# Where slab 0's reciprocal root is computed, and in what order the first loads and matmul pieces are asked for

## Chip, core and metric

The kernel runs on one core of one Trainium2 chip. The core has five engines that run their own instruction queues: TensorE (PE in the profile, with its weight loads as PEld), VectorE (DVE), ScalarE (ACT), GpSimd (POOL) and SyncE (SP), whose queue issues the DMAs here. An engine's queue is in order: an instruction that waits holds up all that stand behind it. The metric is the device time of one execution in microseconds (us); three runs of the kernel before lay within 0.02% of each other.

## The reference, cut to what matters

```python
def reference(A_x, A_w_r, A_w_i, B_x, B_w_gate, B_w_up, B_w_down):
    xn = _layernorm(A_x, axis=-1)                       # (1, 2048, 640), eps 1e-5
    s = irfft2(rfft2(xn) * (A_w_r + 1j * A_w_i))        # spectral filter over both axes
    g = _silu((_gelu(xn @ B_w_gate) * (xn @ B_w_up)) @ B_w_down)   # 640 -> 1536 -> 640
    return A_x + s * g
```

All inputs are bf16. The layer norm of each row (640 elements) needs the row's mean and variance, then 1/sqrt(variance + 1e-5).

## The kernel before, in words

The 2048 rows are cut into 16 slabs of 128 rows (slab n1 holds the rows n1, n1+16, ...), each a tile of 128 partitions by 640 elements in the buffer `X`. Four slabs make a group; a group's normalised rows are transposed into `xnT[g]` (five chunks of 128 columns). The feed-forward part runs tile by tile of 128 of the 1536 hidden columns: for tile t a *gate piece* is five matmuls into a PSUM buffer `psg` (one per chunk), which ScalarE turns into `ge` by gelu, and an *up piece* is five matmuls into `psu`, which VectorE multiplies by `ge` into `uT` (line 795). `psg` and `psu` have two buffers each, so the third gate piece in a row can't begin before the gelu of the first has read its buffer, and likewise for up pieces and their products. Afterwards come the down projection (line 814) and, woven between, the spectral part: folds on VectorE, DFT matmuls, and trips through DRAM. The order of all work is written out by hand: a list `back` of feed-forward pieces and a list `plan` of the other work attached to each.

The change touches the first 11 us alone. There, SP's queue asks for the loads in this order: x of slab 0, the gate weights of tiles 0 to 2 (480 KB), x of slab 1 (160 KB), the up weights of tile 0 (160 KB), the up weights of tiles 1 and 2 (320 KB), x of slabs 2 and 3, then further weights. TensorE runs idle matmuls (`warm_pe`, line 590) on a constant tile until data is there: 19 before the first transposes, and two after them. Slab 0 goes through these steps:

- `stats(0)`: two `bn_stats` of 320 columns each (line 183) and a `bn_aggr` (line 188) on VectorE.
- `root(0, 1)`: VectorE adds 1e-5 (`ve`, line 197), GpSimd raises to the power -0.5 (line 199).
- `inv_consts()`: nine tiny VectorE instructions on 128x1 columns (line 255), constants that are used much later.
- `norm_parts(0)`: VectorE normalises 384, then 256 columns (line 205).
- `slab_Tparts(0)`: three, then two transposes on TensorE into a PSUM tile (line 849), and a copy of each part into `xnT` (line 850). Both copies of slab 0 are ScalarE's; of slab 1's, ScalarE has the first and VectorE the second.

`stats(1)` stands between `norm_parts(0)` and the transposes, then `root(1, 1)`, `inv_rest()` (five tiny VectorE instructions that depend on one another) and the first entries of `back`. Written as g0, u0 for the gate and up piece of tile 0, TensorE's order for slab 0 is g0 g1 u0 g2, transposes of slab 1, u1 u2; and for slab 1 g0 g1 u0 g2 u1 u2. From tile 3 on, gate and up pieces cover two slabs at a time (256 columns), in the order g u g u. ScalarE's function table for gelu is loaded by its first instruction (line 215), while nothing else is there to do.

Of the kernel before, what the change touches and what calls it, by code (L numbers as in the profile page):

```python
# [12 lines left out]
ACT = mybir.ActivationFunctionType  # L13
# [19 lines left out]
def kernel(  # L33
# [40 lines left out]
    with tc.manual_schedule():  # L74
        build(nc, locals())


def build(nc, env):
# [5 lines left out]
    def load_x(n0, n, eng=nc.sync):  # L84
        eng.dma_start(out=X[:, n0:n0 + n, :], in_=xv[:, n0:n0 + n, :])

    def load_w(k, t0, t1):
        f0, f1 = t0 * P, t1 * P
        nc.sync.dma_start(out=(Wg, Wu)[k][:, :, f0:f1], in_=(wgv, wuv)[k][:, :, f0:f1])

    def load_gu(t0, t1):
        for k in range(2):
            load_w(k, t0, t1)

    load_x(0, 1)
    load_w(0, 0, 3)
    load_x(1, 1)
    load_w(1, 0, 1)
    load_w(1, 1, 3)
    load_x(2, 2)  # L100
    load_gu(3, 5)
    load_gu(5, 7)
# [63 lines left out]
    def c1(name, dt=FP32):  # L166
        return consts.tile([P, 1], dt, name=name)

    done = set()
    mva = {}  # L170
    rstd = {}
# [7 lines left out]
    def half_stats(n1, k):  # L179
        if k == 0:  # L180
            st_n[n1] = work.tile([P, 2, nc.vector.BN_STATS_DIM], FP32, tag="st", bufs=3, name="st")
        st = st_n[n1]
        nc.vector.bn_stats(out=st[:, k, :], in_=X[:, n1, 320 * k:320 * k + 320])  # L183
        if k == 1:
            g = n1 // 4
            if g not in mva:
                mva[g] = work.tile([P, 4, nc.vector.BN_AGGR_DIM], FP32, tag="mva", bufs=2, name=f"mva{g}")
            nc.vector.bn_aggr(out=mva[g][:, n1 % 4, :], in_=st)

    def stats(n1):  # L190
        for k in range(2):
            half_stats(n1, k)

    def root(n0, n):
        m = mva[n0 // 4][:, n0 % 4:n0 % 4 + n, :]
        ve = work.tile([P, 4], FP32, tag="ve", name="ve")[:, 0:n]
        nc.vector.tensor_scalar(out=ve, in0=m[:, :, 1], scalar1=1e-5, scalar2=None, op0=ALU.add)  # L197
        r = work.tile([P, 4], FP32, tag="rst", bufs=4, name="rst")[:, 0:n]
        nc.gpsimd.tensor_tensor(out=r, in0=ve, in1=mhalf[:, 0:n], op=ALU.pow)  # L199
        rall[n0] = r  # L200
        for k in range(n):
            rstd[n0 + k] = r[:, k:k + 1]

    def norm(n1, c0=0, c1_=D):
        nc.vector.tensor_scalar(out=X[:, n1, c0:c1_], in0=X[:, n1, c0:c1_], scalar1=mva[n1 // 4][:, n1 % 4, 0:1],
                                scalar2=rstd[n1], op0=ALU.subtract, op1=ALU.mult)
        if c1_ == D:
            done.add(("n", n1))
# [3 lines left out]
    negpi = c1("negpi")  # L212
    nc.vector.memset(negpi, -PI_SAFE)
    warm = c1("warm")
    nc.scalar.activation(out=warm, in_=negpi, func=ACT.Gelu_apprx_tanh)
    b_0, b_1 = c1("b_0"), c1("b_1")
    nc.vector.memset(b_0, 320.0)
    nc.vector.memset(b_1, 0.0)
# [34 lines left out]
    def affine(name, src, a, b):  # L253
        t = c1(name)
        nc.vector.tensor_scalar(out=t, in0=src, scalar1=float(a), scalar2=float(b), op0=ALU.mult, op1=ALU.add)
        return t
# [7 lines left out]
    def fma(name, src, k, add, dt=FP32):  # L264
        t = c1(name, dt)
        nc.vector.scalar_tensor_tensor(out=t, in0=src, scalar=float(k), in1=add, op0=ALU.mult, op1=ALU.add)
        return t
# [8 lines left out]
    def times(name, src, k, by):  # L276
        t = c1(name)
        nc.vector.scalar_tensor_tensor(out=t, in0=src, scalar=k, in1=by, op0=ALU.mult, op1=ALU.mult)
        return t
# [18 lines left out]
    def inv_consts():  # L298
        i_0 = affine("i_0", pf, 4.0, 0.0)
        i_1 = affine("i_1", pf, 4.0, 4.0)  # L300
        i_2 = affine("i_2", pf, 4.0, 2.0)
        o_0 = affine("o_0", pf, 2.0, 320.0)
        o_1 = affine("o_1", pf, 2.0, 2.0)
        o_2 = affine("o_2", pf, 2.0, 321.0)
        o_3 = affine("o_3", pf, 2.0, 1.0)
        ab.extend([(i_0, o_0), (i_1, o_1), (i_2, o_2), (i_2, o_3)])
        kc.append(affine("l_s", s_f, 2.0, 256.0))
        kc.append(affine("hk", h_f, -2.0, 1.0))

    def inv_rest():  # L310
        cq, l_s, hk = kc
        l_k = fma("l_k", h_f, 2.0, l_s)
        l_r = fma("l_r", times("lh", hk, 1.0, hi_f), 1.0, l_k)
        i_r = affine("i_r", l_r, 2.0, 0.0)
        o_r = fma("o_r", l_r, 1.0, cq)
        ab.append((i_r, o_r))
# [1 line left out]
    fwd_consts()  # L318
    vt_iota(0)
    stats(0)  # L320
    root(0, 1)
    inv_consts()

    def tinv_phase(h):
        sl = slice(8 * h, 8 * h + 8)
# [260 lines left out]
    def warm_pe(n):  # L586
        if not warm_bank:
            warm_bank.append(bank(0))
        for _ in range(n):
            nc.tensor.matmul(warm_bank[0][:, 0:256], lhsT=ones[:, 0:P], rhs=ones, start=True, stop=True)  # L590
# [180 lines left out]
    def bank(k):  # L771
        return psA.tile([P, 512], FP32, tag="gu"[k], name="ps" + "gu"[k])
# [55 lines left out]
        for t, k in tk:  # L828
            ffn_piece(0, t, k, j * P, j * P + P)

    GG, REST = ((0, 0), (1, 0)), ((0, 1), (2, 0))

    def run(*items):
        for it in items:
# [2 lines left out]
    PARTS = ((0, 3), (3, 5))  # L837

    def norm_parts(n1):
        for a, b in PARTS:  # L840
            norm(n1, a * P, b * P)

    def slab_Tparts(n1):
        if n1 == 0:
            xnT[0] = xg.tile([P, 5, 512], BF16, tag="xg", name="xnT0")
        for (a, b), ev in zip(PARTS, (nc.scalar.copy, nc.scalar.copy if n1 == 0 else nc.vector.tensor_copy)):
            pt = psB.tile([P, 5, P], BF16, tag="b")
            for c in range(a, b):
                nc.tensor.transpose(out=pt[:, c, :], in_=X[:, n1, c * P:(c + 1) * P], identity=ident)
            ev(out=xnT[0][:, a:b, n1 * P:n1 * P + P], in_=pt[:, a:b, :])  # L850
        done.add(("T", n1))

    NP = 8
    back = [(run, (ffn_slab, 0, GG), (norm_parts, 1), (vt_iota, 1), (ffn_slab, 0, REST), (slab_Tparts, 1),
             (ffn_slab, 0, ((1, 1), (2, 1))),
             (half_stats, 2, 0)),
            (run, (ffn_slab, 1, GG + REST[:1]), (half_stats, 2, 1), (root, 2, 1), (ffn_slab, 1, REST[1:])),
            (run, (ffn_slab, 1, ((1, 1), (2, 1))), (norm, 2), (stats, 3), (root, 3, 1))]
    for h in range(2):
        for t in range(0 if h else 3, NP):  # L860
            back.append((ffn_part, 0, t, h))
# [9 lines left out]
    def put(s, *item):  # L871
        plan[s].append(item)

    put(5, norm, 3)
    put(5, slab_T, 2, 1)
    put(6, slab_T, 3, 0)
# [81 lines left out]
    for i, (n0, n) in enumerate(DG):  # L958
        a = vs0 + 7 * i
# [10 lines left out]
            if (n0 + k) % 2 and 1 < (n0 + k + 3) // 2 < 8:  # L970
                put(min(d + (5 + k if n == 3 else 2), vs0 + 41), load_xt, (n0 + k + 3) // 2)

    warm_pe(19)
    norm_parts(0)
    stats(1)
    slab_Tparts(0)
    warm_pe(2)
    root(1, 1)
    inv_rest()

    put(5, phase_const)
# [36 lines left out]
```

## Time and profile before

| | us |
|---|---|
| median of three runs (202.99 to 203.03) | 203.01 |
| the profiled execution | 203.26 |
| its span, first to last instruction | 201.5 |
| TensorE busy in it | 193.4 |
| VectorE busy | 132.2 |
| ScalarE busy | 122.7 |
| GpSimd busy | 37.4 |

The granted TensorE clock was 0.998 of full speed over the span. TensorE is busy 96% of the span; what it is not busy is mostly in the first 15 us. In the profile, an instruction group is named by its line, its engine, its operation and what it writes and reads (`uT<-psu,ge`); a bracket gives the idle time of the engine just before it and what ended that idle time.

### The profile page before, as it was taken

What the parts mean: (1) busy time and instruction counts of PE and PEld (TensorE: products, weight loads), DVE (VectorE), ACT (ScalarE), POOL (GpSimd) and SP (SyncE); (2) the same over time, 40 slices, a digit from 0 to 9 for tenths busy, and PEclk for the clock granted to TensorE, in tenths of its full rate; (3) what the DMA queues carried; (4) which work ended last, traced back from release to release, by engine and by line L of the source; (5) the groups of instructions that cost most, each with busy time, mean ns of one, the idle gap of its engine ahead of it and who ended that gap; (6) DMA issues with size and microseconds to landing.
All of it is one profiled execution on the core that took longest, in us unless ns stands there. A gap on an engine that the chain in (4) does not pass through costs nothing.

```text
span 201.5 us, 4153 instructions
## 1 busy us (share of the span) xinstructions
PE 193.4 (96%) x1534; PEld 118.6 (59%) x1549; DVE 132.2 (66%) x320; ACT 122.7 (61%) x217; POOL 37.4 (19%) x62
## 2 busy tenths in 40 slices
PE   7889999999999997999999999999999999999993
PEld 5678854777555554576643433457765555556773
DVE  7876869799698784132665557423239786878673
ACT  2447657966967763733688787623564757476632
POOL 5427769999001000000000000000000000000000
PEclk9999999999999999999999999999999999999999
DMA  6999998656669537427982022249900406142512
GB/s 170 332 313 305 387 314 166 130 144 241 156 148 149 134 91 307 121 65 223 322 201 85 25 98 98 109 122 276 282 1 27 140 22 206 36 130 45 186 64 69
DMA packets 40325, 32.44 MB, mean 161 GB/s; under 512 B 15088, under 2 KB 38256, under 8 KB 40048
## 3 DMA queue, kind: packets, MB, share of 16 engines
q1 hardware_dynamic: 40304, 32.17, 55.8%
q8 instruction: 12, 0.20, 0.4%
q14 instruction: 9, 0.07, 0.2%
HBM read 19.03 MB, written 7.88 MB: 134 GB/s over the span
## 4 chain that ended last, share of the span: by engine, by line
PE 64%; DVE 1%; issue 1%; ACT 0%; DVEq 0%
PE psu L789 16%; PE psg L789 16%; PE psg L814 10%; PE psu L814 10%; PE pv L706 2%; PE pd L553 2%; PE pu L653 2%; PE px L626 2%; PE pd L574 1%; PE pd L557 1%; PE pz L543 1%; DVE uT L795 0%; PE pd L576 0%; DVE y L479 0%; ACT G L819 0%
## 5 line engine op out<-in xcount | busy, mean ns | idle before, releaser
L789 PE MATMUL psu<-xnT,Wu 128*128 128x512 bf16 (+2 forms) x289 | 61.0, 339 | 0.9 <-DVE uT L795 0.3
L789 PE MATMUL psg<-xnT,Wg 128*128 128x512 bf16 (+2 forms) x286 | 60.4, 338 | 0.8 <-ACT xnT L850 0.2
L795 DVE TENSOR_TENSOR uT<-psu,ge 128x512 bf16<-128x512 f32 (+2 forms) x59 | 34.4, 587 | 27.8 <-PE psu L789 22.1
L793 ACT ACTIVATE ge<-psg 128x512 bf16<-128x512 f32 (+2 forms) x59 | 30.5, 518 | 27.5 <-PE psg L789 24.6
L814 PEld LDWEIGHTS <-uT 128*128 128x128 bf16 x396 | 37.3, 98 | 14.3 <-issue 0.4
L789 PEld LDWEIGHTS <-Wu 128*128 128x128 bf16 x295 | 26.7, 98 | 23.3 <-issue 3.2
L789 PEld LDWEIGHTS <-Wg 128*128 128x128 bf16 x295 | 26.7, 98 | 21.7 <-issue 1.8
L814 PE MATMUL psg<-Wd,uT 128*128 128x320 bf16 (+1 forms) x204 | 30.7, 294 | 0.0
L814 PE MATMUL psu<-Wd,uT 128*128 128x320 bf16 (+1 forms) x192 | 28.7, 296 | 0.0
L638 DVE TENSOR_TENSOR X<-xs,W 128x972 bf16<-128x972 bf16 (+2 forms) x22 | 13.3, 648 | 10.2 <-ACT xs L634 9.3
L579 ACT CAST zd<-pd 128x660 bf16<-128x660 f32 x16 | 11.3, 706 | 5.5 <-PE pd L576 4.3
L183 DVE BATCH_NORM_STATS2 st<-X 128x6 f32<-128x320 bf16 x32 | 14.1, 477 | 0.4 <-DMA X<-in_A_x_dram 0.3
L708 ACT CAST W<-pv 128x640 bf16<-128x640 f32 x16 | 11.1, 695 | 5.0 <-PE pv L706 5.0
L731 ACT ACTIVATE W<-pd 128x960 bf16<-128x960 f32 (+2 forms) x14 | 10.1, 780 | 5.6 <-PE pd L557 5.5
L545 ACT CAST GEN<-pz 128x640 bf16<-128x640 f32 x16 | 11.2, 702 | 3.1 <-PE pz L543 3.1
L659 ACT CAST X<-pu 128x486 bf16<-128x486 f32 (+4 forms) x22 | 12.3, 558 | 0.3
L634 ACT CAST xs<-px 128x972 bf16<-128x972 f32 (+2 forms) x11 | 10.3, 937 | 2.9 <-PE px L626 2.9
L823 DVE SCALAR_TENSOR_TENSOR G<-th,psg 128x320 bf16<-128x320 f32 x8 | 3.9, 488 | 11.4 <-ACT th L822 11.4
L199 POOL TENSOR_TENSOR rst<-ve,mhalf 128x1 f32<-128x1 f32 (+1 forms) x7 | 5.4, 767 | 23.0 <-DVE ve L197 23.0
L737 DVE TENSOR_TENSOR W<-W 128x960 bf16<-128x960 bf16 (+1 forms) x12 | 6.9, 599 | 3.9 <-ACT W L731 3.8
L764 DVE TENSOR_TENSOR Yall<-Yall,G 128x640 bf16<-128x640 bf16 (+3 forms) x19 | 8.2, 434 | 1.6 <-ACT G L819 1.3
L765 DVE TENSOR_TENSOR Yall<-Yall,xt 128x640 bf16<-128x640 bf16 (+3 forms) x19 | 8.3, 439 | 0.7
(134 smaller groups left out, 207.9 us busy)
## 6 DMA issues: line engine op xcount, KB each, us to landing
W<-W SPq DMA_DIRECT2D x4, 642.0 KB, 5.1
ZDR<-zd SPq DMA_DIRECT2D x32, 80.2 KB, 2.6
xt<-in_A_x_dram SPq DMA_DIRECT2D x8, 320.0 KB, 3.8
UDR<-X SPq DMA_DIRECT2D x10, 240.8 KB, 2.5
out_dram<-Yall SPq DMA_DIRECT2D x14, 160.0 KB, 2.4
B<-ZDR SPq DMA_DIRECT2D x8, 240.8 KB, 4.2
W<-UDR SPq DMA_DIRECT2D x4, 481.5 KB, 6.6
X<-in_A_x_dram SPq DMA_DIRECT2D x3, 640.0 KB, 6.9
```

The costliest lines, as they stand in the source:

```text
L183: nc.vector.bn_stats(out=st[:, k, :], in_=X[:, n1, 320 * k:320 * k + 320])
L545: nc.scalar.copy(out=Zt[n1], in_=pz)
L579: nc.scalar.copy(out=zd.rearrange("p c (q e) -> p c q e", e=10), in_=pd[:, :, 0:330].rearrange("p c (e q) -> p c q e", q=33))
L634: nc.scalar.copy(out=xs, in_=px[:, :, 0:n * w].rearrange("p k (h l) -> p k h l", l=w))
L638: nc.vector.tensor_tensor(out=pp[-1], in0=xs, in1=WT[:, :, h0:h0 + n, l0:l0 + w], op=ALU.mult)
L659: nc.scalar.copy(out=us[:, :, :, c0:c0 + (w + 1 - m) // 2], in_=pv[:, :, :, m:w:2])
L708: nc.scalar.copy(out=vs, in_=pv)
L731: nc.scalar.activation(out=eo[:, b, :, a0:a1].rearrange("p k a n -> p a k n"), in_=py[b][:, a0:a1], func=ACT.Copy, scale=(2.0 if silu[a0] ...
L789: nc.tensor.matmul(ps, lhsT=WT[:, c, t * P:(t + 1) * P], rhs=xnT[g][:, c, c0:c1_], start=(c == 0), stop=(c == 4))
L793: nc.scalar.activation(out=ges[t], in_=ps, func=ACT.Gelu_apprx_tanh)
L795: nc.vector.tensor_tensor(out=uT[g][:, t, c0:c1_], in0=ps, in1=ges[t], op=ALU.mult)
L814: nc.tensor.matmul(ph, lhsT=uT[g][:, t, j * P:(j + 1) * P], rhs=Wd[:, t, c0:c1_], start=(t == 0), stop=(t == NT - 1))
```

## The change

1. Loads: x of slab 1 is asked for second, before the gate weights of tiles 0 to 2; the up weights of tiles 0 to 2 come in one transfer of 480 KB, where there were two.
2. Root of slab 0: one ScalarE instruction, `Abs_reciprocal_sqrt` of the variance with 1e-5 as its bias, in place of VectorE's addition and GpSimd's power. ScalarE's first instruction now loads the table for this function, and a one-column gelu right behind the root loads the gelu table. One constant column (`eps`) is new.
3. VectorE's order: the first half of `stats(1)` moves ahead of `norm_parts(0)`, the second half behind the copy of slab 0's first part. `inv_consts()` moves from behind the root of slab 0 to behind the root of slab 1, just before `inv_rest()`.
4. The copies of slab 0: VectorE has the first part (384 columns), ScalarE the second.
5. TensorE's order: slab 0 is g0 g1 g2 u0 u1, transposes of slab 1, u2; slab 1 is g0 g1 g2 u0 u1 u2. 17 idle matmuls stand before the first transposes, five behind them.

```diff
     load_x(0, 1)
-    load_w(0, 0, 3)
     load_x(1, 1)
-    load_w(1, 0, 1)
-    load_w(1, 1, 3)
+    load_gu(0, 3)
     load_x(2, 2)
...
+    def root_act(n1):
+        rstd[n1] = c1("rst0")
+        nc.scalar.activation(out=rstd[n1], in_=mva[n1 // 4][:, n1 % 4, 1:2], func=ACT.Abs_reciprocal_sqrt, bias=eps)
+        nc.scalar.activation(out=warm, in_=negpi, func=ACT.Gelu_apprx_tanh)
...
     warm = c1("warm")
-    nc.scalar.activation(out=warm, in_=negpi, func=ACT.Gelu_apprx_tanh)
+    eps = c1("eps")
+    nc.vector.memset(eps, 1e-5)
+    nc.scalar.activation(out=warm, in_=eps, func=ACT.Abs_reciprocal_sqrt)
...
     stats(0)
-    root(0, 1)
-    inv_consts()
+    root_act(0)
+    half_stats(1, 0)
...
-    GG, REST = ((0, 0), (1, 0)), ((0, 1), (2, 0))
+    GG, UU = ((0, 0), (1, 0), (2, 0)), ((0, 1), (1, 1), (2, 1))
...
-        for (a, b), ev in zip(PARTS, (nc.scalar.copy, nc.scalar.copy if n1 == 0 else nc.vector.tensor_copy)):
+        evs = (nc.scalar.copy, nc.vector.tensor_copy)
+        for (a, b), ev in zip(PARTS, evs[::-1] if n1 == 0 else evs):
...
-    back = [(run, (ffn_slab, 0, GG), (norm_parts, 1), (vt_iota, 1), (ffn_slab, 0, REST), (slab_Tparts, 1),
-             (ffn_slab, 0, ((1, 1), (2, 1))),
+    back = [(run, (ffn_slab, 0, GG), (norm_parts, 1), (vt_iota, 1), (ffn_slab, 0, UU[:2]), (slab_Tparts, 1),
+             (ffn_slab, 0, UU[2:]),
              (half_stats, 2, 0)),
-            (run, (ffn_slab, 1, GG + REST[:1]), (half_stats, 2, 1), (root, 2, 1), (ffn_slab, 1, REST[1:])),
-            (run, (ffn_slab, 1, ((1, 1), (2, 1))), (norm, 2), (stats, 3), (root, 3, 1))]
+            (run, (ffn_slab, 1, GG + UU[:1]), (half_stats, 2, 1), (root, 2, 1), (ffn_slab, 1, UU[1:2])),
+            (run, (ffn_slab, 1, UU[2:]), (norm, 2), (stats, 3), (root, 3, 1))]
...
-    warm_pe(19)
+    warm_pe(17)
     norm_parts(0)
-    stats(1)
     slab_Tparts(0)
-    warm_pe(2)
+    half_stats(1, 1)
+    warm_pe(5)
     root(1, 1)
+    inv_consts()
     inv_rest()
```

## The prediction, made before the result was known

> **What bounds the kernel now.** I read the page first, then the windows by stage, then the timeline of each engine over the first 15 us. The page's first part and the windows (columns: the window, its length, then busy us of PE, PEld, DVE, ACT, POOL, the granted clock, DMA share, GB/s) say where TensorE is not full:
>
> ```profile
> PE 193.4 (96%) x1534; PEld 118.6 (59%) x1549; DVE 132.2 (66%) x320; ACT 122.7 (61%) x217; POOL 37.4 (19%) x62
> ```
>
> ```profile
> 0.00:5.00 5.00, 3.83 (x19) 2.72 (x19) 3.64 (x38) 1.49 (x2) 2.50 (x10) 1.00 0.60 169
> 5.00:15.00 10.00, 8.79 (x103) 7.08 (x102) 8.27 (x32) 4.82 (x14) 3.35 (x8) 1.00 1.10 323
> 15.00:68.00 53.00, 52.42 (x412) 35.01 (x414) 42.91 (x99) 38.42 (x69) 31.07 (x44) 1.00 0.80 211
> ```
>
> From 15 us on TensorE is full (52.42 of 53 us, and 119.39 of 123.5 after 78). So the change is worth what it moves the moment from which TensorE runs without holes. The timeline of PE shows that moment: its last hole is ahead of the up piece at 14.67, and the lines at 8.32, 11.13 and 12.18 wait for VectorE too.
>
> ```profile
> 6.65 0.82 PE L789 MATMUL psg<-xnT,Wg 128*128 128x128 bf16 x10 [0.23 <-ACT xnT L850]
> 8.32 0.54 PE L849 MATMUL pt<-ident,X 128*128 128x128 bf16 x5 [0.29 <-DVE X L205]
> ...
> 11.13 0.44 PE L789 MATMUL psu<-xnT,Wu 128*128 128x128 bf16 x5 [0.31 <-DVE uT L795]
> ...
> 14.67 0.71 PE L789 MATMUL psu<-xnT,Wu 128*128 128x256 bf16 x5
> ```
>
> What the piece at 14.67 needs is a `psu` buffer, which the product of tile 3 gives back. The timeline of DVE shows that product last in one long chain that begins at 10.79:
>
> ```profile
> 7.05 0.15 DVE L197 TENSOR_SCALAR ve<-mva 128x1 f32<-128x1 f32 x1
> ...
> 7.89 0.64 DVE L205 TENSOR_SCALAR X<-X,mva,rst 128x384 bf16<-128x384 bf16 x2
> ...
> 10.79 0.29 DVE L795 TENSOR_TENSOR uT<-psu,ge 128x128 bf16<-128x128 f32 x1 [0.56 <-PE psg L789]
> 10.99 0.48 DVE L183 BATCH_NORM_STATS2 st<-X 128x6 f32<-128x320 bf16 x1
> ...
> 12.59 0.45 DVE L205 TENSOR_SCALAR X<-X,mva,rst 128x640 bf16<-128x640 bf16 x1 [0.27 <-POOL rst L199]
> 12.95 0.88 DVE L183 BATCH_NORM_STATS2 st<-X 128x6 f32<-128x320 bf16 x2
> 13.87 0.21 DVE L188 BATCH_NORM_AGGREGATE mva<-st 128x2 f32<-128x12 f32 x1
> 14.11 0.15 DVE L197 TENSOR_SCALAR ve<-mva 128x1 f32<-128x1 f32 x1
> 14.19 0.76 DVE L795 TENSOR_TENSOR uT<-psu,ge 128x256 bf16<-128x256 f32 x2
> ```
>
> From the first product of slab 1 (10.79) to the end of the first one at 14.19 it is 3.83 us of instructions that the change leaves in their order. **The forecast is therefore the start of slab 1's first product, against 10.79.** What comes earlier counts only as far as it moves that.
>
> **Part by part.** Times are us of the profiled span.
>
> *Root.* Before: aggregate done 4.26, `ve` 0.15, POOL's power 4.53 to 5.11, norm at 5.14. After: ScalarE's 128x1 instruction. Nearest rows: the 128x1 at 2.01 took 0.20; 128x66 with pointers for scale and bias took 0.43 (two in 0.76). I take 0.30, as one pointer lies between: root done 4.60. Meanwhile VectorE runs half of slab 1's statistics (0.48, next slot at 4.59). Norm at 4.63, 0.51 earlier (bounds 4.59 and 4.73). The new `eps` memset (0.06) goes into VectorE's 0.33 of idle time ahead of 3.13.
>
> *Loads.* x of slab 1 landed 4.2 after its issue at 1.65, 0.42 behind the gate weights (1.18 + 4.3). Second in the queue it lands 0.42 behind slab 0's (0.72 + 2.4), near 3.5; at the 177 GB/s that DMA moved from 2 to 3 us it would be 4.0. It is needed at 4.18: hidden. The gate weights now land third with the same bytes as slab 1's x had, 5.86; needed at 6.36. The 480 KB of up weights follow at 291 to 353 GB/s (the windows from 5 to 10 us): 7.3 to 7.5; the two transfers of before ended at 7.78 (2.68 + 5.1). I take 7.45. One issue (0.53 on SP) goes; all behind it on SP moves up, but lands by bytes: x of slabs 2 and 3 (8.6 before) is needed at 9.5.
>
> *Table load behind the root.* It lies on ScalarE between the root and the copy of slab 0's second part. The load at line 793 stands in the timeline of ACT like this:
>
> ```profile
> 51.36 0.71 ACT L545 CAST GEN<-pz 128x640 bf16<-128x640 f32 x1
> 52.09 1.28 ACT L793 ACT_TABLE_LOAD   x1
> 53.38 0.60 ACT L793 ACTIVATE ge<-psg 128x512 bf16<-128x512 f32 x1
> ```
>
> The instruction before ends at 52.07, the next starts 0.01 behind the load: 1.28 in all. After: load 4.60 to 5.89, gelu 0.20, copy (0.38, overlapping by 0.10 as at 6.12) 6.00 to 6.38. VectorE's copy of 384 columns is 0.36 (between 0.29 for 256 and 0.48 for 640): transposes at 5.07 (0.44 behind the norm, as before), copy 5.64 to 5.99. Five idle matmuls hold TensorE to 6.36 (two at 0.21, three at 0.11: the spacing halves at 5.98). So g0 starts 6.36 against 6.65, and passes its fourth chunk at 6.52 against 6.93. The load is covered, with 0.14 to spare. A switch that cost more would delay g0 by the rest, of which 0.26 more is absorbed ahead of slab 1's transposes.
> The Trainium skill, "ScalarE: Activation LUTs", section "What ACT_TABLE_LOAD costs", speaks against this: it adds about 1.38 of drain to the 1.28, some 2.66 a switch. This trace shows the 1.28 and no drain. By the page g0's fourth chunk would come near 7.8 and the sum would be +1.1, where the row gives +0.1.
>
> *Slab 1's statistics and norm.* The second half runs behind VectorE's copy, 5.91 to 6.39, aggregate 6.43, `ve` 6.67 (before 7.05): 0.38 earlier, POOL's result at 7.47. But now all fourteen tiny constants stand between `ve` and the norm. Before, nine (4.36 to 4.99) lay under slab 0's power, and five (7.12 to 7.79) under slab 1's. Together: nine at 0.06, then five with their dependences, last one started 7.82. Norm(1) starts 7.88 against 7.89: the 0.38 is gone. Bounds: 7.48, POOL's result, and 7.95.
>
> *Order of pieces.* A piece is 0.28, a gelu of 128 columns 0.28.
> Slab 0: g0 to 6.64, g1 to 6.91, g2 waits for the gelu of g0 (6.84 to 7.12) until 7.17, u0 7.50 (weights), u1 to 8.05. Transposes of slab 1: 8.31 against 8.32. Behind them u2 needs u0's buffer, whose product runs 8.44 to 8.73 behind the norm: u2 8.79. ScalarE's copy of slab 1 8.68 to 9.16, so g0 of slab 1 at 9.22 against 9.26. The piece that was done ahead is lost again in waiting.
> Slab 1: g1 9.50; g2 must wait for the gelu of g0 (9.70 to 9.98): 10.03, a hole of 0.25 that the old order filled with u0. So u0 runs 10.31 (before 9.82) and is ready at 10.77 (before 10.27); its product, 0.09 later, at 10.86.
>
> *The idle time at 10.79.* VectorE was free at 10.22 and u0 done at 10.27, so this product could have run at 10.34; it ran at 10.79, and the releaser named had nothing to do with it. Counted in the trace it is VectorE's 64th instruction, waits included. If the 0.45 belongs to that place in the queue, the changed kernel passes it near 9.5 to 10.0, while it waits for u0 anyway; that is the nearest reading, since it is the only such idle time on VectorE. If it belongs to this instruction, it is paid again (rival 1).
>
> *Sum.* 10.86 against 10.79, 0.07; the same working applied to the old order comes 0.02 below the trace at this place, so I take +0.10. All of it reaches 14.67 and so the end. Profiled execution 203.26 + 0.10 = 203.36; the median stands 0.25 under that execution, so 203.01 + 0.10 = **203.11**. Under 0.2% (0.41 us) a measurement of this kernel says nothing, so this is "same".
>
> **The rivals.**
> 1. The idle 0.45 follows the product: 10.77 + 0.5 = 11.28, +0.5: 203.5. For it: nothing in the trace names its cause. Against: the place argument above. Slower once 0.31 of it shows. 22%.
> 2. The up weights land after 8.2, or TensorE's spacing halves 1 to 2 us later than 5.98 since 17 idle matmuls leave it empty from 4.78 to 5.07: each brings +0.3 to +0.6 in all: about 203.5. Against: 7.78 was the worst of before, which had a like hole (5.20 to 5.58). 14%.
> 3. The switch is longer here than its row. It shows from 0.4 over the 1.28 on and makes the kernel slower from 0.7 on; twice the row would put the copy at 7.3 to 7.7, slab 1's g0 at 10.1 and the product at 11.75: +1.0, 204.0. Against: the row at 52.09. 6%. (By the page's 2.66, from the Trainium skill, "ScalarE: Activation LUTs", it would be 204.1.)
> 4. The constants don't hold the norm (7.48): transposes behind u1 at 8.1, the product 0.2 earlier: 202.9. Still "same". 6%. Should both functions share one table, the load vanishes and nothing moves (g0 is held by idle matmuls): 203.1.
> 5. Faster by over 0.2% needs the product by 10.37, so rival 4 and no hole at g2 in slab 1, or a gain later, at the 0.96 hole at 77.23, which is a chain from TensorE's own piece and moves with it: 202.5. 10%.
>
> **Chances and range.** The forecast has 42%. Same: 42 + 6 = 48%; slower: 22 + 14 + 6 = 42%; faster 10%. The likeliest alone: 202.95 to 203.3 (root 0.20 to 0.40, weights up to 7.8). The range takes in rivals 1, 4 and most of 2 and leaves out 3, 5 and the tail of 2: 202.75 to 203.75.
>
> **What would show it.** Right: norm(0) near 4.6, table load 1.28 behind the root, first gate piece near 6.4, norm(1) again near 7.9 with the tiny constants ahead of it, a hole of about 0.25 in slab 1 before g2, the first product of slab 1 near 10.9 and the up piece of tile 5 near 14.8. Wrong: a first product before 10.4 or after 11.2, a copy of slab 0 that waits on the load, or a changed hole at 77.

## The result, and the profile after

The changed kernel takes 203.57 us (median of ten runs, 203.31 to 203.87), the kernel before 203.03 beside it: ratio 1.0024, 95% interval 1.0014 to 1.0033. It is slower by 0.54 us, clear of noise. The forecast was 203.11 and "same"; the time lies in its range and outside the likeliest case's own, and it is past the 0.41 us below which the prediction called a difference nothing. The profiled execution took 203.55 (before 203.26), its span is 201.7 (before 201.5), and from 15 us on TensorE is as full as it was. First the page's first part and then the window from 15 to 68 us (columns as in the prediction):

```profile
PE 194.1 (96%) x1535; PEld 119.1 (59%) x1550; DVE 132.2 (66%) x321; ACT 124.1 (62%) x219; POOL 36.8 (18%) x61
```

```profile
15.00:68.00 53.00, 52.50 (x411) 35.03 (x413) 42.86 (x100) 38.51 (x70) 31.13 (x45) 1.00 0.87 213
```

The timeline of PE after. In the order of lines: g0 to g2 of slab 0, u0 and u1, slab 1's transposes, u2, g0 to g2 of slab 1, u0 and u1, and the up piece of tile 5, which stood at 14.67 before:

```profile
6.52 1.36 PE L794 MATMUL psg<-xnT,Wg 128*128 128x128 bf16 x15
7.83 0.73 PE L794 MATMUL psu<-xnT,Wu 128*128 128x128 bf16 x10
8.40 0.44 PE L855 MATMUL pt<-ident,X 128*128 128x128 bf16 x5
8.74 0.44 PE L794 MATMUL psu<-xnT,Wu 128*128 128x128 bf16 x5
9.30 1.24 PE L794 MATMUL psg<-xnT,Wg 128*128 128x128 bf16 x15
10.38 0.72 PE L794 MATMUL psu<-xnT,Wu 128*128 128x128 bf16 x10
...
14.82 0.71 PE L794 MATMUL psu<-xnT,Wu 128*128 128x256 bf16 x5 [0.16 <-DVE uT L800]
```

The root on ScalarE is done at 4.48 and the table load follows it at once, in the timeline of ACT:

```profile
4.18 0.30 ACT L204 ACTIVATE rst<-mva,eps 128x1 f32<-128x1 f32 x1 [1.96 <-DVE mva L186]
4.49 1.28 ACT L205 ACT_TABLE_LOAD   x1
5.79 0.20 ACT L205 ACTIVATE warm<-negpi 128x1 f32<-128x1 f32 x1
5.90 0.35 ACT L856 COPY xnT<-pt 128x256 bf16<-128x256 bf16 x1
```

In the timeline of DVE norm(1) (L208) starts at 7.79, right behind the last tiny constant `o_r`, though GpSimd's power was done at 7.34. The first product of slab 1 stands at 10.93:

```profile
7.72 0.15 DVE L271 SCALAR_TENSOR_TENSOR o_r<-l_r,cq 128x1 f32<-128x1 f32 x1
7.79 0.63 DVE L208 TENSOR_SCALAR X<-X,mva,rst 128x384 bf16<-128x384 bf16 x2
...
10.93 0.29 DVE L800 TENSOR_TENSOR uT<-psu,ge 128x128 bf16<-128x128 f32 x1 [0.95 <-ACT ge L798]
```

The weights are the surprise. DMA issues from 0 to 6 us (size, median us from issue to landing): the gate weights, issued at 1.64, landed at 6.38, and the up weights, issued at 2.11, at 7.78.

```profile
Wg<-in_B_w_gate_dram SPq DMA_DIRECT2D x1, 480.0 KB, 4.7
Wu<-in_B_w_up_dram SPq DMA_DIRECT2D x1, 480.0 KB, 5.7
```

So the three up pieces of slab 0 begin when the weights land (u0 at 7.83), and slab 1's transposes follow u0 and u1 at 8.40. Norm(1), which the transposes had waited for before, is no longer what they wait for.

### The profile page after: what moved, and what is told of

Same layout as the page of the kernel before. It is cut to its first block, busy times and chain, and to the rows that moved or that the text cites. A ratio compares the mean times of both kernels' runs of the same rounds, so it can differ in the third digit from the quotient of the medians.

```text
span 201.7 us, 4156 instructions
## 1 busy us (share of the span) xinstructions
PE 194.1 (96%) x1535; PEld 119.1 (59%) x1550; DVE 132.2 (66%) x321; ACT 124.1 (62%) x219; POOL 36.8 (18%) x61
## 3 DMA queue, kind: packets, MB, share of 16 engines
HBM read 19.03 MB, written 7.88 MB: 133 GB/s over the span
## 4 chain that ended last, share of the span: by engine, by line
PE 64%; DVE 1%; issue 1%; ACT 0%; DVEq 0%
PE psu L794 16%; PE psg L794 16%; PE psg L819 10%; PE psu L819 9%; PE pv L711 2%; PE pd L558 2%; PE pu L658 2%; PE px L631 2%; PE pd L579 1%; PE pd L562 1%; PE pz L548 1%; DVE uT L800 0%; PE pd L581 0%; DVE y L484 0%; ACT G L824 0%
## 5 line engine op out<-in xcount | busy, mean ns | idle before, releaser
L197 POOL TENSOR_TENSOR rst<-ve,mhalf 128x1 f32<-128x1 f32 (+1 forms) x6 | 4.8, 804 | 23.4 <-DVE ve L195 23.4
```

## The experiments

Two landmarks are used throughout. *T1* is the start of slab 1's transposes on TensorE; *P* is the start of the up piece of tile 5, the last with a hole ahead of it in the first 15 us; the largest hole behind it, at 77 us, is 0.96 long in the kernel before and in the changed one alike. In all profiles but one, the execution's time is P plus 188.6 to 188.8 us, so P is where the time is decided. Landings are the moment at which the last part of a transfer was done. Each ratio has runs of the kernel before on the same chip beside it (there 203.10 to 203.18 in the median).

| kernel | T1 waits for | T1 | T1 to P | P | median us | ratio, 95% |
|---|---|---|---|---|---|---|
| before | norm(1) | 8.32 | 6.35 | 14.67 | 203.03 | 1 |
| changed | up weights | 8.40 | 6.42 | 14.82 | 203.57 | 1.0024 (1.0014 to 1.0033) |
| e9_after (changed, again) | up weights | 8.51 | 6.42 | 14.93 | 203.75 | 1.0033 (1.0021 to 1.0045) |
| e1_shift | norm(1) | 8.14 | 5.93 | 14.07 | 202.84 | 0.9983 (0.9975 to 0.9992) |
| e11_two | norm(1) | 8.11 | 5.94 | 14.05 | 202.79 | 0.9989 (0.9978 to 0.9999) |
| e7_place | up weights | 8.49 | 6.85 | 15.34 | 203.96 | 1.0045 (1.0032 to 1.0057) |
| e2_order | up weights | 8.52 | 5.90 | 14.42 | 203.22 | 0.9999 (0.9990 to 1.0007) |
| e5_root | norm(1) | 8.77 | 5.94 | 14.71 | 202.89 | 0.9992 (0.9983 to 1.0001) |
| e6_root_order | u0 and u1 | 8.30 | 6.43 | 14.73 | 203.41 | 1.0015 (1.0006 to 1.0024) |
| e10_loads | up weights | 8.39 | 5.89 | 14.28 | 203.07 | 1.0000 (0.9991 to 1.0008) |
| e12_oneup | norm(1) | 8.07 | 5.93 | 14.00 | 202.88 | 0.9990 (0.9981 to 0.9998) |
| e8_early | up weights | 8.18 | 6.43 | 14.61 | 203.67 | 1.0024 (1.0015 to 1.0034) |
| e3_consts | up weights | 8.51 | 6.42 | 14.93 | 205.11 | 1.0091 (1.0078 to 1.0104) |
| e4_split | up weights | 9.30 | 6.43 | 15.73 | 204.07 | 1.0037 (1.0025 to 1.0049) |

The stretch from T1 to P takes only four values: 5.89 to 5.94 with the old order of pieces, 6.42 to 6.43 with the new, and some 0.42 more on either where the idle time at VectorE's 64th place falls on the product of slab 1 (before, e7_place). (T1, P and the landings are those of the profiled execution, which in e5_root, e4_split and the kernel before was later than the median.) The changed kernel was run once more beside e10_loads, e11_two and e12_oneup:

> The changed kernel as it is, beside the three others here on one chip. Both theories: ratio 1.0024 (203.6), up piece of tile 5 at 14.7 to 14.9.

It came out at 203.75, 0.15 over the expectation, with the interval of its ratio overlapping the first one. Its up piece of tile 5 came at 14.93, 0.03 past the expected range.

**The idle 0.45 of the kernel before: a place in the queue?** e1_shift puts one memset that nothing reads at VectorE's start, so the product becomes its 65th instruction.

```diff
     warm = c1("warm")
+    spare = c1("spare")
+    nc.vector.memset(spare, 1e-5)
```

> The kernel before with one more VectorE instruction, a memset of an unused 128x1 column next to `warm`, in VectorE's idle time ahead of 3.13 us. Theory (the 0.45 us of idle time ahead of slab 1's first product belongs to the place in VectorE's queue, its 64th instruction counted with the waits): the 64th is now the wait ahead of the product, it is passed while TensorE still works on u0, the product runs near 10.35 instead of 10.79, and the kernel takes about 0.4 us less, 202.6. Rival (the idle time belongs to the product itself, or to something else on the chip): idle time still 0.4 to 0.5 at the product, time unchanged within 0.1 us, 203.0.

The product ran at 10.19, and the time fell to 202.84. The timeline of DVE in e1_shift has no idle time ahead of it:

```profile
9.55 0.49 DVE L183 BATCH_NORM_STATS2 st<-X 128x6 f32<-128x320 bf16 x1
10.19 0.29 DVE L797 TENSOR_TENSOR uT<-psu,ge 128x128 bf16<-128x128 f32 x1
```

e7_place asks the reverse of the changed kernel: one instruction fewer on VectorE, so that the product is the 64th again.

```diff
-    nc.vector.memset(eps, 1e-5)
+    nc.gpsimd.memset(eps, 1e-5)
```

> The changed kernel with the memset of eps on GpSimd, so that VectorE has one instruction less and the first product of slab 1 is its 64th again. Theory A (the idle 0.45 follows the place and counts from the instruction ahead): product at 11.3 to 11.4 instead of 10.93, up piece of tile 5 near 15.2, 204.0, ratio 1.004 to 1.005. Theory B (it counts from an earlier moment and has passed while VectorE waits for TensorE here): product at 10.93, 203.57, ratio 1.002.

Theory A held: u0 of slab 1 was ready when VectorE's wait for it ended at 10.96, and the product ran at 11.44.

```profile
11.44 0.29 DVE L800 TENSOR_TENSOR uT<-psu,ge 128x128 bf16<-128x128 f32 x1 [1.37 <-PE psu L794]
```

e11_two is e1_shift with a second memset, which tells a place in the queue from a mere delay:

```diff
     nc.vector.memset(spare, 1e-5)
+    nc.vector.memset(spare, 1e-5)
```

> The kernel before with two extra memsets instead of one. Theory (the idle 0.45 belongs to VectorE's 64th place, which now falls on an instruction that no one waits for): as with one memset, product at 10.2, ratio 0.998. Rival (the extra memset helped by moving the work behind it): the second moves it again, by 0.1 or more either way.

As with one memset; and the idle time can be seen where it went. The statistics instruction ahead of the product is now the 64th and starts at 9.78 (9.55 in e1_shift), with idle time that nothing in the trace released:

```profile
9.78 0.49 DVE L183 BATCH_NORM_STATS2 st<-X 128x6 f32<-128x320 bf16 x1 [0.16 <-issue]
10.19 0.27 DVE L798 TENSOR_TENSOR uT<-psu,ge 128x128 bf16<-128x128 f32 x1
```

The start of the 64th instruction is 0.46 to 0.48 behind that of the 63rd in all three traces that show the idle time (before, e7_place, e11_two). In e11_two 0.21 is usual between these two instructions, so the statistics are 0.25 late, and the product behind them isn't.

So the place is shown. Why the 64th instruction waits is not.

**The order of pieces.** e2_order is the changed kernel with the old order of gate and up pieces.

```diff
-    GG, UU = ((0, 0), (1, 0), (2, 0)), ((0, 1), (1, 1), (2, 1))
+    GG, REST = ((0, 0), (1, 0)), ((0, 1), (2, 0))
...
-    back = [(run, (ffn_slab, 0, GG), (norm_parts, 1), (vt_iota, 1), (ffn_slab, 0, UU[:2]), (slab_Tparts, 1),
-             (ffn_slab, 0, UU[2:]),
+    back = [(run, (ffn_slab, 0, GG), (norm_parts, 1), (vt_iota, 1), (ffn_slab, 0, REST), (slab_Tparts, 1),
+             (ffn_slab, 0, ((1, 1), (2, 1))),
...
```

> The changed kernel with the old order of pieces (g0 g1 u0 g2, transposes of slab 1, u1 u2; slab 1 g0 g1 u0 g2 u1 u2). Theory (the new order costs the hole ahead of g2 in slab 1 and puts u0 one piece later): the hole at 10.10 goes, the first product of slab 1 comes at about 10.4 instead of 10.93, the up piece of tile 5 near 14.3 instead of 14.82, the kernel about 0.5 us faster than the changed one: near 203.05. Rival (the weights that land at 7.78 set the pace whatever the order): under 0.2 us gained.

T1 was 0.12 later than in the changed kernel's profile, with the up weights (7.90), and P 0.40 earlier; 203.22, against 203.57 to 203.75. The product came at 10.52 (expected 10.4). The time is 0.17 over the expectation, but the kernel before was 0.15 slower beside it too (203.18), and the ratio fell by 0.0025 to 0.0034, which is the 0.5 us that was expected or a little more.

**The root alone, and the order on top of it.** e5_root is e1_shift with the root on ScalarE and the table load (`root_act` as in the change), and nothing else of it; e6_root_order adds the new order.

```diff
     spare = c1("spare")
     nc.vector.memset(spare, 1e-5)
-    nc.scalar.activation(out=warm, in_=negpi, func=ACT.Gelu_apprx_tanh)
+    eps = c1("eps")
+    nc.vector.memset(eps, 1e-5)
+    nc.scalar.activation(out=warm, in_=eps, func=ACT.Abs_reciprocal_sqrt)
...
     stats(0)
-    root(0, 1)
+    root_act(0)
```

> The kernel before with the extra memset and, of the change, only the root of slab 0 on ScalarE with the gelu table behind it; old loads, old order of pieces, constants where they were. Theory (the root and the table load cost nothing, and what is won in norm(0) is lost in waiting for norm(1)): norm(0) near 4.85 instead of 5.13, transposes of slab 1 at 8.1 to 8.2 as with the memset alone, that product at 10.15 to 10.25, ratio 0.998 (202.85). Rival (the switch of tables costs by itself): the first gate piece later than 6.5, the product at 10.4 or later, ratio 0.999 to 1.000.

> As e5_root, and the changed kernel's order of pieces besides, with the old loads. Theory (the order costs 0.4 by itself: the product of slab 1 stands one gate piece and one wait for the gelu later): product near 10.6, the up piece of tile 5 near 14.45, ratio 1.000 (203.25). Rival (the order costs only with the late up weights): product at 10.2, ratio 0.998 (202.85).

In e5_root norm(0) started at 4.64, 0.5 earlier than before, and no gain came of it: 202.89, ratio 0.9992, where the memset alone has 0.9983 with an overlapping interval. In the profiled execution x of slab 1 landed late (6.29) and T1 waited for it, as the timeline of PE shows:

```profile
8.77 0.54 PE L858 MATMUL pt<-ident,X 128*128 128x128 bf16 x5 [0.68 <-DVE X L210]
```

So its T1, and the product behind it (10.82), missed the expectation, for a reason that lies in the landing and not in the root. The new order on top of it cost 0.52 (203.41), 0.1 more than expected and as much as the stretch from T1 to P grew (0.49). Its product came at 10.84 and P at 14.73, both 0.25 or so later than expected, because the transposes stand behind u0 and u1 there (T1 8.30). The order costs this with the old loads, so it does not need late weights.

**The loads.** e10_loads is e1_shift with the changed loads alone; e12_oneup takes only the single transfer of the up weights.

```diff
     load_x(0, 1)
-    load_w(0, 0, 3)
     load_x(1, 1)
-    load_w(1, 0, 1)
-    load_w(1, 1, 3)
+    load_gu(0, 3)
```

```diff
     load_w(0, 0, 3)
     load_x(1, 1)
-    load_w(1, 0, 1)
-    load_w(1, 1, 3)
+    load_w(1, 0, 3)
```

> The kernel before with the extra memset and, of the change, the loads alone (x of slab 1 second, gate and up weights of tiles 0 to 2 in one transfer each). Theory (the loads cost what the order of pieces does not): gate weights landed at 6.1 to 6.5, up weights at 7.6 to 7.9, the first up piece at 7.9, slab 1's transposes at 8.5, the product at 10.5, ratio 1.000 (203.2), 0.35 over the memset alone. Rival (the late weights are hidden behind norm(1), which ends no earlier here): transposes at 8.2, product at 10.2, ratio 0.998.

> The kernel before with the extra memset and the up weights of tiles 0 to 2 in one transfer instead of two, gate weights still second and x of slab 1 third. If the one transfer is what makes the loads dear: gate weights at 5.1 to 5.5 as before, up weights at 7.5 to 7.8, the first up piece 0.2 to 0.4 later, transposes at 8.3 to 8.5, ratio 0.999 to 1.000. If the place of x of slab 1 is: as with the memset alone, ratio 0.998.

With the changed loads u0 waits for the up weights (landed 7.77), and T1 for u0 and the gate piece behind it. Both lines are from the timeline of PE of e10_loads:

```profile
7.82 0.45 PE L789 MATMUL psu<-xnT,Wu 128*128 128x128 bf16 x5 [0.59 <-DMA Wu<-in_B_w_up_dram]
...
8.39 0.44 PE L849 MATMUL pt<-ident,X 128*128 128x128 bf16 x5
```

With the single transfer alone the up weights landed at 6.95, earlier than in any other kernel, and u0 waited for nothing. The timeline of PE of e12_oneup:

```profile
7.10 0.44 PE L790 MATMUL psu<-xnT,Wu 128*128 128x128 bf16 x5
...
8.07 0.34 PE L850 MATMUL pt<-ident,X 128*128 128x128 bf16 x3 [0.25 <-DVE X L204]
```

On one chip the loads cost 0.28 against e11_two (203.07 against 202.79) and 0.19 against e12_oneup (202.88), which has the single transfer too. The intervals of the ratios overlap; T1 of the profiled executions tells the kernels apart (8.39, against 8.11 and 8.07). What costs is that x of slab 1 goes ahead of the gate weights. The same bytes stand ahead of the up weights in e10_loads and e12_oneup, and yet their first part landed 0.23 later in e10_loads and their last 0.82 later.

e2_order, above, has the root, the order on VectorE, the swapped copies and the idle matmuls of the change besides these loads. It has the ratio of e10_loads (0.9999 against 1.0000) and the same stretch from T1 to P (5.90 against 5.89). So those parts, taken together, show no cost and no gain.

e4_split, the changed kernel with the up weights in two transfers again, agrees that the single transfer isn't what costs:

```diff
-    load_gu(0, 3)
+    load_w(0, 0, 3)
+    load_w(1, 0, 1)
+    load_w(1, 1, 3)
```

> The changed kernel with the up weights of tiles 0 to 2 in two transfers again (tile 0, then tiles 1 and 2); x of slab 1 stays second. Theory (the single transfer's landing at 7.78 sets u0): tile 0's weights land near 7.0, u0 starts right behind g2 at about 7.72 instead of 7.83, u1 waits for the second transfer near 7.9 to 8.0; slab 1's transposes 8.25 to 8.4, gain 0 to 0.15 us. Rival (the single transfer is the better one, the small one of 256 B runs slows all): u1 later than 8.15, time 0.1 to 0.3 us longer than the changed kernel.

It was no faster (204.07). In its profile the gate weights landed at 7.22 and the up weights at 7.90 and 8.96, with T1 at 9.30.

**The constants.** e8_early moves the nine constants ahead of slab 0's statistics; e3_consts moves all fourteen behind the first pieces of the plan.

```diff
     vt_iota(0)
+    inv_consts()
     stats(0)
...
     root(1, 1)
-    inv_consts()
     inv_rest()
```

```diff
     root(1, 1)
-    inv_consts()
-    inv_rest()
...
+    put(5, inv_consts)
+    put(6, inv_rest)
```

> The changed kernel with the nine constants of inv_consts ahead of the statistics of slab 0 instead of ahead of norm(1). Theory (not the constants but the up weights hold slab 1's transposes): norm(0) 0.2 to 0.3 later, norm(1) at 7.3 to 7.5 instead of 7.79, transposes of slab 1 still behind the up weights at 8.4 or later, ratio 1.002 (203.57). Rival (the constants gate it): the transposes and the product 0.3 to 0.4 earlier, ratio 1.0005 (203.2).

> The changed kernel with the fourteen tiny constants of `inv_consts` and `inv_rest` put off to the feed-forward steps of tiles 5 and 6, where VectorE has idle time. Theory (up weights that land at 7.78 hold u0 and u1 and through them slab 1's transposes at 8.40): norm(1) starts near 7.4 instead of 7.79, the transposes stay near 8.4, the time stays within 0.15 us of the changed kernel. Rival (the constants ahead of norm(1) hold slab 1, as the prediction had it): transposes near 8.0 and 0.3 us gained.

Norm(1) started at 7.54 and at 7.32 instead of 7.79, and both times T1 stayed 0.61 and 0.62 behind the up weights' landing (7.57 and 7.89). So the constants hold norm(1), and norm(1) no longer holds the transposes: e8_early has the ratio of the changed kernel. e3_consts was far slower for another reason, in the place that the constants went to. The timeline of DVE, of POOL and of PE of e3_consts:

```profile
18.15 1.01 DVE L283 SCALAR_TENSOR_TENSOR lh<-hk,pb 128x1 f32<-128x1 f32 x1
19.20 0.68 DVE L271 SCALAR_TENSOR_TENSOR l_r<-lh,l_k 128x1 f32<-128x1 f32 x1
19.91 0.15 DVE L260 TENSOR_SCALAR i_r<-l_r 128x1 f32<-128x1 f32 x1
19.98 0.73 DVE L271 SCALAR_TENSOR_TENSOR o_r<-l_r,cq 128x1 f32<-128x1 f32 x1
```

```profile
16.79 2.37 POOL L331 TENSOR_SCALAR GEN<-GEN,u,ph_t 128x1024 int32<-128x1024 int32 x2 [1.63 <-DVE ph_t L271]
19.12 0.74 POOL L367 TENSOR_SCALAR GEN<-GEN 128x660 f32<-128x660 f32 x1
```

```profile
21.09 0.70 PE L794 MATMUL psu<-xnT,Wu 128*128 128x256 bf16 x5 [1.06 <-DVE uT L800]
```

Instructions that take 0.15 in the changed kernel took 0.68 to 1.01 here, and the product behind them left a hole of 1.06 on TensorE, the largest of its new ones. This is the one kernel whose time is not P plus 188.7.

**The fastest version** is the kernel before with one or two idle memsets: ratio 0.9983 and 0.9989, with overlapping intervals. None of the parts of the change that were tried on top of the memset (root, loads, single transfer, root and order) improved it.

## Why the prediction was right, and where it was not

- *The forecast rests on the start of slab 1's first product: right.* It was to come at 10.86 and came at 10.93, and the executions followed P in every kernel but e3_consts. That T1 came so near to its forecast (8.40 for 8.31) is in part luck, since it came by another wait: the up weights and not norm(1). Luck has a part in the range too. It reached to 203.75 for the sake of rivals 1 and 2, which stood at 203.5, and neither came as it was written.
- *Root and table load: right.* 0.30 and 1.28 as taken; norm(0) at 4.51 instead of 4.63. The load was over before the weights of g0 were there and cost nothing. The 2.66 of the Trainium skill, "ScalarE: Activation LUTs", section "What ACT_TABLE_LOAD costs", did not show: ScalarE's idle time was under 0.02 on either side of the load, with the gelu behind it at 5.79. Here the measurement decides.
- *The constants take norm(1)'s gain: right* (7.79 for 7.88). Rival 4 hoped for 0.2 without them. It let the transposes wait for u1, at 8.1, and reckoned with the early landing of the up weights; with the late one there is nothing to gain, as e8_early shows.
- *Order of pieces: right.* The hole ahead of g2 of slab 1 came (10.10 for 10.03), and u0 behind it. The order was worth +0.50 by the stretches and 0.52 by e5_root and e6_root_order. In the forecast this cost does not stand out, because it is set off against the next term.
- *The idle 0.45 belongs to the 64th place: right*, in both directions (e1_shift, e7_place). It was worth 0.42 in the stretch from T1 to P and 0.34 in the median of e1_shift. Rival 1 needed only one VectorE instruction fewer: e7_place, at 203.96.
- *Loads: wrong in size.* The gate weights landed at 6.38 for 5.86, the up weights at 7.78 for 7.45, at the edge of the likeliest case's range. The prediction moved landings by bytes. The first part of the gate weights did land about as late as that (5.11, against 4.52 to 4.76 with the old loads), but the last came 1.27 behind it (before 0.93, in e1_shift 0.41). Rival 2 put its bound at 8.2 for the up weights; in fact T1 is their landing plus 0.62, so against the 8.31 of the prediction they count from 7.7 on. The other half of rival 2 came in this execution and cost nothing: the idle matmuls stood 0.21 apart up to the last (6.31), the spacing halved near 6.8, and the last matmul of g2 (7.66) still started before the up weights were there. In e9_after it was 0.11 from 5.36 on.
- *"The median stands 0.25 under that execution, so 203.01 + 0.10": this step failed.* Of the 0.46 that the forecast missed, 0.05 came up to P (0.15 later for 0.10), 0.14 lies behind P or outside the span (the profiled executions differ by 0.29), and 0.27 is this offset, which the forecast took to hold for the changed kernel. But the kernel before has a span of 201.3 to 201.4 in the median of its runs beside the experiments and 201.5 in its profile, so most of the offset lay inside the span. The timelines of DVE point to T1. In the kernel before, slab 1's statistics start 0.03 behind the landing of their x (5.86), though norm(0) was done at 5.78; in e1_shift that x landed at 5.68, and they follow norm(0) at once. First the kernel before, then e1_shift:

```profile
5.89 0.89 DVE L183 BATCH_NORM_STATS2 st<-X 128x6 f32<-128x320 bf16 x2
```

```profile
5.70 0.89 DVE L183 BATCH_NORM_STATS2 st<-X 128x6 f32<-128x320 bf16 x2
```

  T1 followed that landing by 2.46 to 2.53 in before, e1_shift, e11_two and e5_root. It was 0.2 earlier in e1_shift and e11_two, where x landed at 5.68 and 5.58; in e5_root, where x landed at 6.29, the profiled execution stood 0.44 over its median. The changed kernel's T1 hangs on the up weights instead and does not get the 0.2 back; its profile stood 0.02 under its median. That x usually lands earlier in the kernel before than in its one profile is inferred and not shown.

Added up over the medians: the 64th place -0.34 (e1_shift), the loads +0.28 (e10_loads against e11_two), the order +0.52 (e6_root_order against e5_root), together +0.46; measured +0.54. The root is left out: e5_root stood 0.21 below its before where the memset alone stood 0.34 below its own, and the intervals of the two ratios overlap.

## What to carry to other kernels

Before you add a trace's offset from the median to a forecast, ask which wait made that execution late, and whether the change leaves that wait in place. A wait that nothing in the trace releases may belong to a place in an engine's queue: one idle instruction ahead of it shows this, and may be worth more than the change. And a load that is moved ahead of another may delay it by more than its own bytes, as here, so price the transfer behind it by its last part.

## What the runs showed of the hardware

- VectorE's 64th instruction, waits counted, started late by 0.41 in the kernel before (10.30 to 10.79, less the usual 0.07 between a wait and its product), by 0.41 in e7_place (10.96 to 11.44) and by 0.25 in e11_two. In e1_shift and in the changed kernel it fell on the wait ahead of the product and cost nothing. It is no rule for every program: in e3_consts the 64th, a wait at 14.38 behind VectorE work without a hole, shows no idle time, and neither do the 128th and the 192nd of the kernel before, each 0.03 behind the end of the one ahead.
- Transfers of 480 KB end raggedly. From the first part done to the last it was 0.3 to 0.4 for the gate weights in e1_shift, e6_root_order, e11_two and e12_oneup, 0.9 and 1.2 in the kernel before and e5_root, which have the loads of e1_shift, and 0.9 to 2.1 wherever x of slab 1 went ahead of them. The windows of the changed kernel show the stream slow between x and the weights:

```profile
2.50:3.00 0.50, 0.50 (x4) 0.38 (x3) 0.30 (x6) 0.00 (x0) 0.13 (x1) 1.00 0.96 309
3.00:3.50 0.50, 0.50 (x5) 0.32 (x4) 0.49 (x2) 0.00 (x0) 0.50 (x1) 1.00 0.76 88
3.50:4.00 0.50, 0.50 (x4) 0.38 (x3) 0.47 (x3) 0.00 (x0) 0.39 (x1) 1.00 0.59 183
```

  The last column falls from 309 to 88 and 183 GB/s. In the kernel before the dip between x of slab 0 and the weights is shorter (226, 128, 284 and 315 in the half microseconds from 2.0 to 4.0). What makes the last part late stays open.
- Three tiny VectorE instructions with two tensor inputs took 0.68 to 1.01 instead of 0.15 in e3_consts while GpSimd ran long ones, and the first two ended within 0.01 of GpSimd's instructions. One with one input, between them (19.91), took its 0.15. The Trainium skill, "GPSIMD Engine Reference", section "1. Specifications", says that GpSimd shares its SBUF interface with VectorE and that VectorE's instructions with two SBUF inputs contend for it; this trace agrees, except for one such instruction at 18.08 that took 0.15 beside the same work. The third slow one ended at 20.71, in the middle of an instruction of GpSimd that ran from 19.95 to 22.40.
